# Start of a convolution and maxout kernel: wider weight transfers, one pass for the last 64 channels, and a new order of the opening work

## The chip, the cores and the metric

The kernel runs on one core of a Trainium2 chip. The metric is the device time of one execution in microseconds (us). Where a time stands with "at", it is counted from the start of the profiled span.

The engines are called as the profile calls them: PE (TensorE, matrix products; PEld is its loading of weights), ACT (ScalarE), DVE (VectorE), POOL (GpSimd) and SP (SyncE, which here issues almost all DMAs; its issues are listed as SPq).

## The reference

The input x holds 8 sequences of 4160 tokens with 192 channels. Each group of 24 channels (one head) is convolved along the sequence with its own 7 weights, the softmax of a row of `weight`, looking only backwards. Then every token goes through a feed-forward layer with three candidate products:

```python
w = softmax(weight)                                   # (8 heads, 7 taps)
x_pad = np.concatenate([zeros(B, 6, D), x], axis=1)
out = np.einsum('hk,bskhg->bshg', w, x_unf)           # causal convolution, x_unf: 7 shifted views
h = np.maximum(np.maximum(x @ w1, x @ w2), x @ w3)    # (33280, 768)
return h @ w_out                                      # (33280, 192)
```

All inputs and outputs are 4-byte floats. w1, w2 and w3 are 192 x 768 (590 KB each), w_out is 768 x 192.

## The kernel before

**The algebra.** With y the convolved tokens, max(y w1, y w2, y w3) is max(relu(y(w1-w3)), y(w2-w3)) + y w3. So two products per tile are needed instead of three: one with w1-w3 and one with w2-w3. The part y w3 goes through w_out together with the rest: a small matrix `m16` = w3 w_out is made once. The 192 channels are handled as three chunks of 64. The differences are kept in `wd` (line 305): `wd[:, 0]` and `wd[:, 1]` hold channels 0 to 127 of the two products, `wd[:, 2]` holds channels 128 to 191 of both (one in the lower 64 partitions, one in the upper), and a fourth part is made from the first two by `cross_wd` (L322), which moves 64 partitions to the other half. `make_wd` (L310) subtracts for two of the six 128-wide column groups j at a time.

**The blocks.** The tokens are cut into 65 blocks of 512. For the first four (the "dense" blocks) the convolution is done on PE by `conv_dense` (L376): 5 pieces of up to 103 tokens, each multiplied with a band matrix that holds the taps. From block 4 on, another form of the convolution is used, with transposing DMAs. This study is about the first 25 us; what follows is a steady loop over blocks 2 to 64 (L762).

**`conv_dense`.** The input of a dense block comes in as `xf` (one DMA for a block, two for block 0), is cast to 2-byte floats into `xz` by `cast_dense` (L207; two variants v, three casts each), and is multiplied by 32-channel slots: 4 slots are written beside each other into the 128 PSUM partitions. Pass n=0 does slots 0 to 3 (channels 0 to 127), pass n=1 does slots 4 and 5 (channels 128 to 191) twice, so that both halves of the partitions hold the result, and each pass is copied to `yd` in one copy. `cross` (L395) fills the rest of `yd` for blocks 2 and 3.

**The products of blocks 0 and 1.** `l1_dense` (L527) makes them in two parts. Part "F" multiplies channels 0 to 127 and needs `yd[:, 0]` and `wd[:, 0]`, `wd[:, 1]`. Part "H" multiplies channels 128 to 191 (the "third products") and needs `yd[:, 2]` and `wd[:, 2]`. A pair such as (0, 2), (0, 3) means block 0, column groups 2 and 3. `tops` (L545) then takes a relu on ACT (L500) and a maximum on DVE (L505), which together empty the PSUM tiles.

**The order.** The schedule is written by hand: each engine runs its own instructions in the order of the program text, and waits for the data that an instruction needs. PSUM tiles come from pools with a tag: `psp` ("p") and `psq` ("q") have two buffers each, `psw` ("w") four. A new tile in a pool waits until the tile two (or four) before it has been read.

**The transfers.** All of the opening loads stand in SP's queue (L241 to L250): block 0's x, then slices of the weights by `load_wa` (L227: channels 0 to 127 of w3, w1, w2, three DMAs) and `load_wb` (L231: channels 128 to 191, three DMAs with 64 rows each), block 1's x between them, then w_out and blocks 2 and 3. In order: x0, wa 0:256, wb 0:256, x1, wa 256:512, wb 256:768, wa 512:768, w_out, x2, x3.

**Where the weights are prepared.** `make_wd` of groups 0:2 on DVE (L692, L693, L700), of group 2:4 on DVE for n = 0, 1 (L710, L711) and on POOL for n = 2 (L705), of 4:6 on POOL (L707). `copy_w3` (L314) doubles the upper part of w3 into the other 64 partitions; `cast_w3` (L318) makes the 2-byte w3 that PE transposes in `transpose_w3` (L334). ACT copies the transposed result out (L341), then does one `cross_wd` (L729), its share of block 2's convolution (L393, L399), and the two copies of `make_m` (L349). `make_m` uses both "p" buffers, and the first product of block 2 (L517) takes the first of these two next.

**`zero_x`** (L131) clears rows of the input buffers that blocks 4 to 6 will use, on ACT unless another engine is named.

Of the kernel before, what the change touches and what calls it, by code (L numbers as in the profile page):

```python
# [19 lines left out]
GRP = 24  # L20
BAND_W = 128 + PAD
NBLK = 512
CHK = 103
HALF = P // 2
# [4 lines left out]
def kernel(  # L29
# [12 lines left out]
    nc = tc.nc  # L42
# [3 lines left out]
    H, KWs = weight.shape  # L46
# [193 lines left out]
    wos = const.tile([P, NJ, D], FP32)  # L240
    load_x(0)  # L241
    load_wa(slice(0, PW))
    load_wb(slice(0, PW))
    load_x(1)
    load_wa(slice(PW, 2 * PW))
    load_wb(slice(PW, DFF))
    load_wa(slice(2 * PW, DFF))
    nc.sync.dma_start(out=wos[:], in_=moe_w_out.rearrange("(j p) c -> p j c", p=P))
    load_x(2)
    load_x(3)  # L250
# [1 line left out]
    make_identity(nc, ident[:])  # L252
    ident16 = const.tile([P, P], FP16)
    nc.gpsimd.tensor_copy(out=ident16[:], in_=ident[:])
    idle = const.tile([P, NBLK], FP16)
    nc.vector.memset(idle[:], 0.0)
    def keep_warm(widths, pool, tag):
# [24 lines left out]
    nc.vector.reciprocal(out=wrec[:], in_=wrec[:])  # L282
    zero_x(4)
    nc.vector.tensor_scalar_mul(out=line[0:NHEAD, 31:31 + KW], in0=wexp[:, 0:KW], scalar1=wrec[:])
    for v in range(2):
        nc.vector.memset(xz[1][v][:], 0.0)
    cast_dense(0, (nc.vector.tensor_copy, nc.vector.tensor_copy))
    CUT = 28
    for lo, hi, copy in ((0, CUT, nc.scalar.copy), (CUT, WIN, nc.vector.tensor_copy)):
        bps = psq.tile([32, hi - lo + 3, NHEAD], FP32, tag="q", name=f"band_{lo}")  # L290
        for c in range(lo, hi):
# [4 lines left out]
        for a in range(4):  # L296
            copy(out=band[32 * a:32 * a + 32, :, 32 * a + lo:32 * a + hi],
                 in_=bps[:, 0:hi - lo, :].rearrange("p c h -> p h c"))
    zero_x(5)
    keep_warm((NBLK,) * 3, psp, "p")  # L300


# [70 lines left out]
            slots[t0] = ysp.tile([P, 2, nu, 2, D], FP16, tag="ys", name=f"ys_{t}")  # L373
        convs[t0] = G, heads[0]

    def conv_dense(t, copies, pools=((None, None),) * 2, order=(0, 1)):  # L376


        yd = dense[t] = ydp.tile([P, NC, NBLK], FP16, tag="yd", name=f"yd_{t}")
        for n in order:  # L380
            slots_ = ((0, 1, 2, 3), (4, 5, 4, 5))[n]
            pool, tag = pools[n]
            ps = (pool or psw).tile([P, NBLK], FP32, tag=tag or "w", name=f"D{n}_{t}")
            for (q, b, row_lo, rlen, lo, hi, cc) in chunks_of[t]:
                for v in range(2):
                    for g, s in enumerate(slots_):
                        h = (32 * s + 31 * v) // GRP
                        nc.tensor.matmul(  # L388
                            ps[32 * g:32 * g + 32, lo:hi],
                            lhsT=xz[t][v][0:rlen, q, 32 * s:32 * s + 32],  # L390
                            rhs=band[0:rlen, h, cc:cc + hi - lo],
                            start=(v == 0), stop=(v == 1), tile_position=(0, 32 * g))
            copies[n](out=yd[:, 2 * n, :], in_=ps[:])  # L393

    def cross(t, *copies):  # L395

# [294 lines left out]
    GP = nc.gpsimd.tensor_copy  # L691
    make_wd(0, 0, 2)  # L692
    make_wd(1, 0, 2)  # L693
    zero_x(6, 4, NR, nc.vector)
    conv_dense(0, (ACT, DVE))
    zero_x(6, 0, 4)
    for t in range(NDENSE, XBUF):
        load_x(t)
    copy_w3(DVE, 0, 2)
    make_wd(2, 0, 2)  # L700
    cast_dense(1, (GP, ACT), (1, 2, 0))
    l1_dense([(0, 0, PQ), (0, 1, PQ)], "F")
    cast_w3(0, 2)
    copy_w3(GP, 2, 6)
    make_wd(2, 2, 4, nc.gpsimd)  # L705
    for n in range(NC):
        make_wd(n, 4, 6, nc.gpsimd)  # L707
    cast_w3(2, 6)
    conv_dense(1, (DVE, ACT), order=(1, 0))
    make_wd(0, 2, 4)  # L710
    make_wd(1, 2, 4)  # L711
    cross_wd(0, GP)
    GP(out=wo[:], in_=wos[:])
    l1_dense([(0, 0, PQ), (0, 1, PQ)], "H")
    tops((0, 0), (0, 1))
    l1_dense([(1, 0, WW), (1, 1, WW)], "HF")
    tops((1, 0), (1, 1))
    l1_dense([(0, 2, PQ), (0, 3, PQ)], "FH")
    tops((0, 2), (0, 3))
    l1_dense([(1, 2, WW), (1, 3, WW)], "HF")  # L720
# [5 lines left out]
    tops((1, 4), (1, 5))  # L726
    transpose_w3((PQ[0], PQ[0], PQ[1]))
    cast_dense(3, (GP, GP))
    cross_wd(1, ACT)  # L729
    first_hidden(0)  # L730
    first_hidden(1)
    conv_dense(2, (ACT, DVE), (WW[0], PQ[1]))
    cast_x(4)
    cross(2, ACT, DVE)
    make_m(0)
# [26 lines left out]
    for t in range(2, NB):  # L762
        u = convs_at.get(t, NB)
        late = t > 2 and u < NB
        if t in (3, 4):
            double(t + 1)
        if t > 3:
            for v in range(casts.get(t - 1, 8) + 1, casts[t] + 1):
                cast_x(v)
        l1(t, 0)  # L770
        if t == 2:
            first_rest()
        elif t == 3:
            cast_x(8)
            nc.gpsimd.tensor_copy(out=m16[0:HALF, 2, :], in_=m16[HALF:P, 0, :])
            nc.gpsimd.tensor_copy(out=m16[HALF:P, 2, :], in_=m16[HALF:P, 1, :])
        if t > 3 and not late:
            op(lambda t=t: (store(t - 2, 0, 4, (nc.sync,)),
                            turn(t + 2, (2,)) if place(t + 2)[1:] in ((0, 4), (0, 5)) else None,
                            turn(t + 1, (4,)) if place(t + 1)[1:] == (0, 5) else None, load_on(t)))  # L780
        else:
            op(lambda t=t: store(t - 2, 0, 4, (nc.sync,)))
        cuts = ROOM if late else EVEN
        st2(t - 1, (cuts[0], cuts[0]))
        for j in range(1, NJ):
            l1(t, j)
            if late and j == 1:
                st2(t - 1, (cuts[0] + OWN + AHEAD, cuts[0] + OWN))
                meet()
                quad, second = u >= QUADS, u < QUADS or t == u - 3  # L790
                conv(u, WPWQ, range(4 * second, 4 * second + 4) if quad else range(NHEAD))
                for i in (0, 2):
                    evac(u, i)
                for i in (1, 3):
                    evac(u, i, nc.vector.tensor_copy)
                if second:
                    turn(u)
# [52 lines left out]
```

## Time and profile before

| | |
|---|---|
| median of 3 runs | 453.1 us (452.54, 453.10, 453.47) |
| the profiled execution | 452.5 us |
| its span | 450.7 us, so 1.8 us lie around the span |
| PE busy | 444.7 us (99%) |
| DVE, ACT, POOL busy | 356.5, 320.3, 204.0 us (79%, 71%, 45%) |
| granted clock of PE | 1.00 |
| DMA | 72.01 MB, mean 160 GB/s |

Three rows of the opening, as the timelines give them:

| engine | from | what |
|---|---|---|
| PE | 6.22 | block 0's convolution, 80 matmuls, 1.10 us |
| PE | 9.87 | block 1's convolution, after a wait of 0.61 us |
| PE | 11.10 | from here on PE is busy without a larger gap |

A line of a timeline has: start, time taken, engine, line of the kernel, operation, tile written <- tiles read, shape, count, and in brackets the idle time before it with what ended it. A busy PE is not a PE at its peak, since matmuls overlap and their ends are modelled. What matters for this study is which wait ends last in a given stretch.

### The profile page before, as it was taken

The numbers are of one execution on the slowest core, as the hardware profiler recorded it, in microseconds if no ns is written. First come the engines' busy times: TensorE is split into PE (matmuls) and PEld (weight loads), VectorE is DVE, ScalarE is ACT, GpSimd is POOL, SyncE is SP. The second block draws the span as 40 slices with busy tenths as digits, with TensorE's granted clock in tenths as the row PEclk, the third lists the DMA queues.
The fourth block names the chain that finished last, engine by engine and source line by source line (L and its number), as shares of the span: only waits on it lengthen the run. The fifth ranks groups of instructions, "written<-read, shape, count | busy, mean of one in ns | idle before, by whom it ended". The sixth has DMA issues, their size and how long they took to land.

```text
span 450.7 us, 18261 instructions
## 1 busy us (share of the span) xinstructions
PE 444.7 (99%) x7576; PEld 409.5 (91%) x7576; DVE 356.5 (79%) x610; ACT 320.3 (71%) x600; POOL 204.0 (45%) x234
## 2 busy tenths in 40 slices
PE   7999999999999999999999999999999999999997
PEld 4579999999999999999999999999999999999996
DVE  7778778878778787787887887887887887887775
ACT  7977677767677676776776777776776776776664
POOL 2874836556464524714724635526544545124000
PEclk9999999999999999999999999999999999999999
DMA  7978999495977759649559749769549566172123
GB/s 204 238 191 158 208 183 240 134 217 148 183 208 161 184 107 214 172 112 205 158 138 185 190 103 193 192 105 218 157 116 207 160 157 151 48 139 75 56 71 106
DMA packets 128242, 72.01 MB, mean 160 GB/s; under 512 B 52320, under 2 KB 127967, under 8 KB 128159
## 3 DMA queue, kind: packets, MB, share of 16 engines
q1 hardware_dynamic: 127999, 70.75, 68.8%
q8 instruction: 59, 0.97, 1.0%
q14 instruction: 24, 0.20, 0.2%
q10 hardware_dynamic: 160, 0.10, 0.1%
HBM read 33.28 MB, written 25.56 MB: 131 GB/s over the span
## 4 chain that ended last, share of the span: by engine, by line
PE 97%; DMA 1%; SPq 1%; issue 0%; DVE 0%; POOL 0%; POOLq 0%
PE po L582 36%; PE lq L517 32%; PE lp L517 22%; PE G L367 3%; PE lw L541 1%; DMA xf<-in_x_dram 1%; PE D L388 1%; PE lp L541 1%; PE po L613 0%; PE po L640 0%; SPq L233 0%; SPq L229 0%; PE pm L347 0%; PE lq L541 0%; SPq L167 0%; PE pt L338 0%
## 5 line engine op out<-in xcount | busy, mean ns | idle before, releaser
L582 PE MATMUL po<-wo,h 64*128 64x192 f16 x3024 | 331.7, 243 | 0.0
L505 DVE TENSOR_TENSOR h<-r,lq 128x512 f16<-128x512 f16 x384 | 263.0, 686 | 84.3 <-ACT r L500 74.3
L500 ACT ACTIVATE r<-lp 128x512 f16<-128x512 f32 x384 | 229.0, 597 | 113.4 <-PE lp L517 103.0
L517 PE MATMUL lp<-yp,wd 64*128 64x512 f16 x1098 | 295.6, 376 | 0.0
L517 PE MATMUL lq<-yp,wd 64*128 64x512 f16 x1098 | 295.5, 376 | 0.0
L582 PEld LDWEIGHTS <-h 64*128 64x128 f16 x3024 | 242.6, 94 | 5.5 <-issue 4.1
L517 PEld LDWEIGHTS <-wd 64*128 64x128 f16 x2268 | 181.6, 94 | 14.9 <-issue 0.2
L199 POOL CAST x<-xf 103x768 f16<-103x768 f32 x122 | 97.2, 825 | 112.4 <-DMA xf<-in_x_dram 108.9
L582 PE MATMUL po<-m,yp 64*128 64x192 f16 x720 | 140.3, 243 | 0.0
L430 POOL COPY yp<-yp 64x1536 f16<-64x1536 f16 (+1 forms) x70 | 90.9, 1298 | 87.3 <-DMA yp<-ys 62.3
L590 DVE TENSOR_TENSOR o<-a,po 128x384 f32<-128x384 f32 x126 | 69.0, 548 | 0.0
L582 PEld LDWEIGHTS <-yp 64*128 64x128 f16 x720 | 66.3, 94 | 0.1
L589 ACT COPY a<-po 128x384 f32<-128x384 f32 x126 | 59.5, 472 | 0.0
L407 ACT CAST ys<-G 128x480 f16<-128x480 f32 (+1 forms) x53 | 25.4, 530 | 9.5 <-PE G L367 9.5
L407 DVE CAST ys<-G 128x480 f16<-128x480 f32 (+1 forms) x53 | 30.2, 610 | 0.0
L367 PE MATMUL G<-x,band 39*32 39x240 f16 (+3 forms) x1024 | 16.5, 242 | 0.0
L367 PEld LDWEIGHTS <-band 39*32 39x32 f16 x1024 | 10.2, 91 | 4.6 <-issue 4.1
L517 PE MATMUL lq<-yd,wd 64*128 64x512 f16 x36 | 9.7, 376 | 0.0
L517 PE MATMUL lp<-yd,wd 64*128 64x512 f16 x36 | 9.7, 376 | 0.0
L541 PEld LDWEIGHTS <-wd 128*128 128x128 f16 (+1 forms) x48 | 3.1, 96 | 6.0 <-issue 2.8
L216 POOL CAST xz<-xf 112x160 f16<-112x160 f32 (+2 forms) x15 | 4.3, 330 | 7.9 <-DMA xf<-in_x_dram 7.8
L388 PEld LDWEIGHTS <-xz 112*32 112x32 f16 x320 | 3.9, 96 | 2.7 <-POOL xz L216 1.1
(79 smaller groups left out, 98.1 us busy)
## 6 DMA issues: line engine op xcount, KB each, us to landing
xf<-in_x_dram SPq DMA_DIRECT2D x113, 234.0 KB
out_dram<-o SPq DMA_DIRECT2D x62, 384.0 KB
wall<-in_moe_w_dram SPq DMA_DIRECT2D x12, 128.0 KB
xf<-in_x_dram SPq DMA_DIRECT2D x7, 204.8 KB
xf<-in_x_dram SPq DMA_DIRECT2D x3, 420.0 KB
yp<-ys SPq DMA_TRANSPOSE x70
out_dram<-o SPq DMA_DIRECT2D x5, 192.0 KB
wos<-in_moe_w_out_dram SPq DMA_DIRECT2D x1, 576.0 KB
```

The costliest lines, as they stand in the source:

```text
L199: nc.gpsimd.tensor_copy(out=x16s[t0][0:K, :, :, u, r, :].rearrange("p h j c -> p j h c"), in_=xf[0:K, 4 * r:4 * r + 4, :].rearrange("p j ( ...
L367: nc.tensor.matmul(G[2 * (k // per) + i][TOK * j:TOK * (j + 1), k % per, :], lhsT=band[row, h, HALF * i + LAP:HALF * i + KR], rhs=x16s[t0] ...
L388: nc.tensor.matmul(ps[32 * g:32 * g + 32, lo:hi], lhsT=xz[t][v][0:rlen, q, 32 * s:32 * s + 32], rhs=band[0:rlen, h, cc:cc + hi - lo], star ...
L407: copy(out=slots[t][:, i % 2, :, :, GRP * h0:GRP * (h0 + per)].rearrange("p u r (h c) -> p h (u r) c", c=GRP), in_=G[i][:].rearrange("p h ...
L430: nc.gpsimd.tensor_copy(out=yp[HALF * i:HALF * (i + 1), 1, :, :, :, :].rearrange("p i u k n -> p (i u k n)"), in_=yp[HALF * (1 - i):HALF * ...
L500: nc.scalar.activation(out=r[:], in_=ps[0][:], func=AF.Relu)
L505: nc.vector.tensor_max(out=hs[t][:, j, :], in0=r[:], in1=q[:])
L517: nc.tensor.matmul(ps[i][:], lhsT=w_of(i, c, j), rhs=y_all(t, i, c), start=(n == 0), stop=(n == NC - 1))
L541: nc.tensor.matmul(open_ps[t, j, i][:], lhsT=a, rhs=b, start=(t, j, i) not in begun, stop=(t, j, i) in begun)
L582: nc.tensor.matmul(ps[b0, i][:, s % 2, :], lhsT=a, rhs=b, start=first, stop=last)
L589: nc.scalar.copy(out=a[:], in_=ps[s - 1, 0][:])
L590: nc.vector.tensor_add(out=outs[t][:, s - 1:s + 1, :], in0=a[:], in1=ps[s - 1, 1][:])
```

## The change

1. **Transfers.** The order becomes x0, wa 0:256, x1, wb 0:768, wa 256:768, w_out, x2, x3. The same bytes come in 9 weight transfers instead of 12: wb in three DMAs of 197 KB (instead of 66 and 131 KB), the later wa in three of 262 KB (instead of six of 131 KB). x1 is ahead of all of wb.
2. **Third chunk once.** Pass n=1 of `conv_dense` multiplies slots 4 and 5 only once per piece; pieces 0 to 2 write the lower 64 partitions, pieces 3 and 4 the upper, in pairs. That makes 60 matmuls per block instead of 80. The two halves (309 and 203 columns) are then copied to `yd` in four copies of 64 partitions: each half once to its own partitions, once to the others (in block 1 the second is done by POOL from `yd`).
3. **Who does what.** `make_wd` of 2:4 and 4:6 is all on POOL; `cast_w3` is one cast of all columns, behind them; both `copy_w3` go to ACT; `cross_wd(0)` goes from POOL to ACT, next to `cross_wd(1)`. Block 1's casts go from POOL and ACT to DVE and POOL. `zero_x(5)` and `zero_x(6)` go from ACT (and DVE) to POOL, as do the memsets of `xz[1]` from DVE. The band's copies are cut at column 25 instead of 28 between ACT and DVE.
4. **Order.** Block 1's convolution stands directly behind block 0's F part in the text, its pass n=0 first; POOL's weight work stands behind it. Block 1's first pair is done "FH" instead of "HF". The loads of x4 to x6 stand later in the text.

```diff
@@ loads
     load_x(0)
     load_wa(slice(0, PW))
-    load_wb(slice(0, PW))
     load_x(1)
-    load_wa(slice(PW, 2 * PW))
-    load_wb(slice(PW, DFF))
-    load_wa(slice(2 * PW, DFF))
+    load_wb(slice(0, DFF))
+    load_wa(slice(PW, DFF))
@@ setup
+    for v in range(2):
+        nc.gpsimd.memset(xz[1][v][:], 0.0)
-    for v in range(2):
-        nc.vector.memset(xz[1][v][:], 0.0)
-    CUT = 28
+    CUT = 25
-    zero_x(5)
+    zero_x(5, eng=nc.gpsimd)
@@ conv_dense
-    def conv_dense(t, copies, pools=((None, None),) * 2, order=(0, 1)):
+    def conv_dense(t, copies, pools=((None, None),) * 2, order=(0, 1), dup=None):
+        ch = chunks_of[t]
+        FAR = (NQ + 1) // 2
         for n in order:
-            slots_ = ((0, 1, 2, 3), (4, 5, 4, 5))[n]
+            if n == 0:
+                units = [[(c, 0, (0, 1, 2, 3))] for c in ch]
+            else:
+                units = [[(c, 2 * (c[0] // FAR), (4, 5)) for c in ch[k::FAR]] for k in range(FAR)]
...
-            copies[n](out=yd[:, 2 * n, :], in_=ps[:])
+            if n == 0:
+                copies[0](out=yd[:, 0, :], in_=ps[:])
+            else:
+                far = ch[FAR][4]
+                for i, (lo, hi) in enumerate(((0, far), (far, NBLK))):
+                    own, other = (slice(HALF * k, HALF * (k + 1)) for k in (i, 1 - i))
+                    copies[1 + i](out=yd[own, 2, lo:hi], in_=ps[own, lo:hi])
+                    if dup is None:
+                        copies[1 + i](out=yd[other, 2, lo:hi], in_=ps[own, lo:hi])
+                    else:
+                        dup(out=yd[other, 2, lo:hi], in_=yd[own, 2, lo:hi])
@@ the hand-written order
     make_wd(1, 0, 2)
-    zero_x(6, 4, NR, nc.vector)
-    conv_dense(0, (ACT, DVE))
-    zero_x(6, 0, 4)
+    conv_dense(0, (ACT, ACT, DVE))
+    cast_dense(1, (DVE, GP), (1, 2, 0))
+    l1_dense([(0, 0, PQ), (0, 1, PQ)], "F")
+    copy_w3(ACT, 0, 2)
+    make_wd(2, 0, 2)
+    copy_w3(ACT, 2, 6)
+    zero_x(6, eng=nc.gpsimd)
+    conv_dense(1, (ACT, DVE, DVE), dup=GP)
+    for n in range(NC):
+        make_wd(n, 2, 4, nc.gpsimd)
+    l1_dense([(0, 0, PQ), (0, 1, PQ)], "H")
+    tops((0, 0), (0, 1))
+    l1_dense([(1, 0, WW), (1, 1, WW)], "FH")
+    tops((1, 0), (1, 1))
+    for n in range(NC):
+        make_wd(n, 4, 6, nc.gpsimd)
+    cast_w3(0, 6)
+    GP(out=wo[:], in_=wos[:])
     for t in range(NDENSE, XBUF):
         load_x(t)
-    copy_w3(DVE, 0, 2)
-    make_wd(2, 0, 2)
-    cast_dense(1, (GP, ACT), (1, 2, 0))
-    l1_dense([(0, 0, PQ), (0, 1, PQ)], "F")
-    cast_w3(0, 2)
-    copy_w3(GP, 2, 6)
-    make_wd(2, 2, 4, nc.gpsimd)
-    for n in range(NC):
-        make_wd(n, 4, 6, nc.gpsimd)
-    cast_w3(2, 6)
-    conv_dense(1, (DVE, ACT), order=(1, 0))
-    make_wd(0, 2, 4)
-    make_wd(1, 2, 4)
-    cross_wd(0, GP)
-    GP(out=wo[:], in_=wos[:])
-    l1_dense([(0, 0, PQ), (0, 1, PQ)], "H")
-    tops((0, 0), (0, 1))
-    l1_dense([(1, 0, WW), (1, 1, WW)], "HF")
-    tops((1, 0), (1, 1))
     l1_dense([(0, 2, PQ), (0, 3, PQ)], "FH")
...
     cast_dense(3, (GP, GP))
+    cross_wd(0, ACT)
     cross_wd(1, ACT)
     first_hidden(0)
     first_hidden(1)
-    conv_dense(2, (ACT, DVE), (WW[0], PQ[1]))
+    conv_dense(2, (ACT, DVE, ACT), (WW[0], PQ[1]))
@@ the loop, at t == 2
-                conv_dense(3, (ACT, DVE))
+                conv_dense(3, (ACT, DVE, ACT))
```

More of the change, by code (lines that the diff above doesn't have):

```diff
@@ L382, in conv_dense @@
             pool, tag = pools[n]
             ps = (pool or psw).tile([P, NBLK], FP32, tag=tag or "w", name=f"D{n}_{t}")
-            for (q, b, row_lo, rlen, lo, hi, cc) in chunks_of[t]:
+            for unit in units:
                 for v in range(2):
[L386 to L392, printed above, removed]
@@ L393, in conv_dense @@
-            copies[n](out=yd[:, 2 * n, :], in_=ps[:])
+                    for (q, b, row_lo, rlen, lo, hi, cc), g0, slots_ in unit:
+                        for g, s in enumerate(slots_, g0):
+                            h = (32 * s + 31 * v) // GRP
+                            nc.tensor.matmul(
+                                ps[32 * g:32 * g + 32, lo:hi],
+                                lhsT=xz[t][v][0:rlen, q, 32 * s:32 * s + 32],
+                                rhs=band[0:rlen, h, cc:cc + hi - lo],
+                                start=(v == 0), stop=(v == 1), tile_position=(0, 32 * g))
```

## The prediction

> **What bounds the kernel now.** I read the page's busy shares first: PE is busy 444.7 of 450.7 us. So nothing can be gained in the steady loop except by giving PE less to do; all else is in the opening. Then PE's timeline there:
>
> ```profile
> 6.22 1.10 PE L388 MATMUL D<-band,xz 112*32 112x103 f16 x80 [0.38 <-DVE band L297]
> 8.24 0.59 PE L541 MATMUL lp<-yd,wd 128*128 128x512 f16 x2 [0.91 <-ACT yd L393]
> 9.87 1.30 PE L388 MATMUL D<-band,xz 112*32 112x103 f16 x80 [0.61 <-POOL xz L216]
> 11.10 0.39 PE L541 MATMUL lp<-yd,wd 64*128 64x512 f16 x1
> ...
> 13.15 0.59 PE L541 MATMUL lp<-yd,wd 128*128 128x512 f16 x2
> ...
> 14.16 0.39 PE L541 MATMUL lp<-yd,wd 64*128 64x512 f16 x1
> ```
>
> PE waits three times and runs through from 11.10 (H of block 0) to the end. The chain of waits says why it is 11.10: x1 is issued at 5.05, lands at 9.36, is cast, and block 1's convolution follows.
>
> ```profile
> 5.05 4.31 DMA xf<-in_x_dram
> ```
>
> Why 4.31 us? The windows (last columns: granted clock, DMA share, GB/s):
>
> ```profile
> 3.50:5.50 2.00, 2.00 (x44) 1.32 (x41) 1.91 (x10) 1.82 (x4) 0.00 (x0) 1.00 0.80 226
> 5.50:7.25 1.75, 1.37 (x82) 0.95 (x80) 1.64 (x7) 1.71 (x3) 0.00 (x0) 1.00 0.72 103
> 7.25:9.25 2.00, 1.09 (x12) 0.38 (x4) 1.71 (x4) 1.75 (x3) 0.00 (x0) 1.00 1.07 343
> 9.25:12.50 3.25, 2.64 (x90) 1.52 (x90) 1.66 (x4) 2.34 (x6) 1.41 (x4) 1.00 0.92 252
> ```
>
> At 103 GB/s the engines are starved: SP needs 0.58 to 0.60 us for each of the three wb issues at 3.15 to 5.01, and each brings only 66 KB (some 110 GB/s).
>
> Two more views set what follows. POOL's timeline gives the price of a weight subtraction, 2.96 us for 4, the first 0.72 (DVE's row: 0.42):
>
> ```profile
> 13.38 2.96 POOL L312 TENSOR_TENSOR wd<-wall 128x256 f16<-128x256 f32 x4 [0.20 <-DMA wall<-in_moe_w_dram]
> 16.29 1.03 POOL L320 CAST w3h<-wall 128x1024 f16<-128x1024 f32 x1
> ```
>
> And ACT, from 17.38 to 25.49, has no idle time over 0.1 us:
>
> ```profile
> 17.38 1.08 ACT L500 ACTIVATE r<-lp 128x512 f16<-128x512 f32 x2 [0.26 <-PE lq L541]
> ...
> 19.80 1.60 ACT L341 CAST w3t<-pt 128x512 f16<-128x512 f32 x3
> 21.42 0.83 ACT L323 COPY wd<-wd 64x768 f16<-64x768 f16 x1
> 22.32 0.59 ACT L393 CAST yd<-D 128x512 f16<-128x512 f32 x1
> 22.93 0.62 ACT L399 COPY yd<-yd 64x512 f16<-64x512 f16 x1
> 23.46 0.71 ACT L349 CAST m<-pm 128x192 f16<-128x192 f32 x2
> ```
>
> The first of these last two copies ends at 23.76 and frees a "p" buffer; PE starts block 2's first product (L517) at 23.81. PE and ACT arrive together there: any ACT work added before it delays PE.
>
> **The change, part by part.**
>
> *x1 and the early order: 1.7 us early, but not on the path.* By the windows 448 KB are moved at 3.50, so x0 and the first wa (823 KB) are through at about 5.2; x1 (430 KB at 343 GB/s) at 6.4, and with the lag that x1 showed before (its last byte by volume at 8.3, landed 9.36) it lands near 7.4 instead of 9.36. Casts on DVE and POOL (before: 0.86 on POOL; DVE's six for block 0 took 0.92, so three 0.46) end by about 8.6 even one after the other. H also needs all of wb: 1843 KB, by volume at about 9, landed 9.4, plus 0.42 for `wd[:, 2]`. H can start at about 9.6 instead of 11.10. The cheaper setup (`zero_x(5)` 1.47 off ACT, memsets 0.92 off DVE, the band's cut) is under these waits: block 0's casts cannot start before x0 is there (before: 4.61, directly behind the memset), and nothing is charged or credited.
>
> *What is late next: wa 256:768, through POOL.* F of (0, 2) needs `wd[:, 0]` and `wd[:, 1]`, H `wd[:, 2]`, now all on POOL and none before the big wa has landed, w3, w1, w2 in that order. Behind x0 and the first wa 1806 KB must come. At 343 GB/s that takes 5.3 us, at 252 it takes 7.2; over 7.25 to 14.00 the windows (343, 252, then 205) average 268, 6.7 us. By volume the end is at 10.5 to 12.4; the lag before was 1.0 us for x1 and about as much for the weights. So w2 lands between 11.5 and 13.4; I take 12.4, nearer to the row in which wb was on its way too (252), and w1 0.9 earlier, 11.5. Then POOL does three subtractions: max(11.5 + 3 x 0.73, 12.4 + 2 x 0.73) + 0.1 = 14.0. H of (0, 2) starts at 14.0 instead of 14.16: **-0.2** (-1.1 to +0.7). Of the 1.5 us won at H of (0, 0) nearly all is waited away here. Queued behind the waiting subtraction on POOL are those of 4:6, the w3 cast, w_out's cast and the casts of blocks 2 and 3: 11.5 + 6 x 0.73 = 15.9, + 1.64 = 17.5, + 1.14 = 18.7, still ahead of PE's transposes (18.80 before) and `first_hidden` (19.55 before). SP waits for POOL's `zero_x` only behind x3, some microseconds later.
>
> *ACT ahead of block 2: +1.15.* The anchor is H of (0, 4) and the relu behind it at 17.38, which move with the -0.2. From there ACT gets `cross_wd(0)`: 0.83 + 0.02. Block 2's convolution adds two copies of 64 x 203. From PSUM copies of 512 and 192 columns (0.586, 0.313) a column costs 0.85 ns, so 0.32 each; neighbours overlap by 0.1 to 0.2 (the relus start every 0.49 and take 0.60), so 0.30 for both. The pair of copies of `make_m` ends its first at 23.76 + 1.15 - 0.2 = 24.7, and PE starts L517 then, +0.95 against 23.81.
>
> *PE's own share: -0.18.* 80 matmuls start within 0.90 us, four at a time every 45 ns. The new pass needs 6 groups of four (the last pair half empty) instead of 10: 0.18 less per block. For blocks 0 to 2 this lies under the waits above; for block 3 (at 26.34, PE without gaps) it counts. ACT's two extra copies there are covered by its idle 1.02 before 28.64; without that cover they would cost up to 0.3. If the pairs do not run beside each other the gain is 0.
>
> *The rest.* The four 64-partition copies of blocks 0 and 1 (ACT 0.41 each, DVE 0.36 each) and POOL's doubling are ahead of the 14.0 with over 1 us to spare. The later loads of x4 to x6 come no later, because the stream before them is not starved any more.
>
> Sum: -0.2 + 1.15 - 0.18 = **+0.75 us**. The profiled execution's 452.5 becomes 453.25; the median is 0.6 higher, so I forecast 453.8 against 453.1.
>
> **Where a rule and a row differ.** The forecast leaves PE idle from about 11.5 to 13. Before, gaps up to 0.91 left the granted clock at 1.00. The Trainium skill, "TensorE: Matmul & The Clock Gate", section "Why this matters for your kernels", wants no gaps over some 3 us, or the clock halves; by that rule a gap of 2 us is safe, and the trace shows no longer one than the first 1.23. The Trainium skill, "DMA: Bandwidth & Descriptors", section "Where 436 GB/s comes from", puts one core's limit from memory at 358 GB/s; at that the 1806 KB would take 5.0 us (an estimate), so the measured 343 is nearly all there is.
>
> **The rivals.**
>
> *Slower: the wide wa is the new wait (0.40).* Mechanism: one 786 KB delivery feeds three 0.73 us subtractions on one engine, where before the same weights came in two portions and DVE did two of the three at 0.42. If wb beside it holds the stream at 252 GB/s or less, w2 lands at 13.4, H starts at 14.96, and the sum is +0.8 + 1.15 - 0.18 = +1.8. It decides from a landing of w2 at about 12.6 on, where the sum passes +0.9. For it: 252 and 205 GB/s in the rows after 9.25. Against it: 343 where nothing starves, 320 at 14 to 16. Price 454.9.
>
> *Faster: the stream runs at its best (0.10).* w2 at 11.0: POOL is done at 12.55, ahead by 1.6, and the sum is -1.6 + 1.15 - 0.18 = -0.6; PE cannot be ready for that H before about 12.25 (11.10 - 9.6 = 1.5, and some 0.3 of own time), so -1.0 is the end. Price 452.3.
>
> *ACT is not the gate at 23.8 (0.15).* If L517's buffer does not wait for `make_m`'s copy, or ACT's copies overlap more, +1.15 falls away and conv 2's 0.18 counts too: -0.2 - 0.36 = -0.55, 452.5. Against it: 23.76 and 23.81.
>
> *Clock gate (0.03).* A gap twice as long as forecast could cost some 3 us at half clock (half of it lost): 455.3.
>
> *The third chunk is not made at half price* (pairs not side by side): +0.18 on the forecast, within it.
>
> **How the numbers follow.** Forecast and its neighbours within 0.9 us (0.32), slower rival 0.40, clock 0.03, faster 0.10, ACT not the gate 0.15. A measurement of this kernel can tell about 0.2%, 0.9 us, from no change. Of the third rival nearly all is within that, as of the forecast's; some of the faster rival is too, since it only touches -0.9. That makes faster 0.12, same 0.46, slower 0.42. The forecast alone reaches from -0.2 to +0.9; with the landing's ends and the rivals' prices the range is 452.3 to 455.1.
>
> **What would show it.** Right: x1's casts near 7.5; block 1's convolution before 9; PE idle before the products of (0, 2), released by POOL's `wd`; no starved window of 100 GB/s; ACT between w3t and the copies of `make_m` longer by 1.1, and PE's L517 released by ACT. Wrong: H of (0, 2) before 13 or after 15; L517 directly behind pm; a convolution of 60 matmuls that still takes 1.1 us; new idle time of PE beyond 30 us.

## The result, and the profile after

After takes 458.49 us (457.95 to 458.77, 4 runs), before 452.82 in the same call (452.47 to 453.47): ratio 1.0116, interval 1.0088 to 1.0143, **5.7 us slower**. The prediction said 453.8, at most 455.1. After's profiled execution took 458.42, span 456.6 against 450.7, of which PE is busy 445.6 (444.7 before): of the 5.9 us between the spans 5.0 are waits of PE and 0.9 more busy time, though it has 80 matmuls fewer.

All that is lost is lost ahead of 66 us. Taking the same relu in both traces and subtracting its start before from its start after gives the clock of the loss: +1.87 at the first (block 0's first products), +2.58 at those of slices 2 to 5, +4.20 at block 2's first, +4.96 behind block 3's convolution, +5.79 from 66 us to the end. So there are four pieces: 2.58 in the opening, 1.62 ahead of block 2, 0.76 at block 3, 0.83 at 65 us.

PE's timeline of after in the opening (start, us, engine, line, in the bracket the idle time before it and what ended it):

```profile
4.84 1.20 PE L291 MATMUL band<-ident,line 128*32 128x32 f16 x38 [1.04 <-DVE line L284]
5.97 1.46 PE L261 MATMUL idle<-idle 128*128 128x512 f16 x3
7.37 1.56 PE L392 MATMUL D<-band,xz 112*32 112x103 f16 x60
...
12.12 0.91 PE L392 MATMUL D<-band,xz 112*32 112x103 f16 x60 [1.85 <-DVE xz L216]
12.97 0.39 PE L555 MATMUL lp<-yd,wd 64*128 64x512 f16 x1
...
15.37 0.60 PE L555 MATMUL lp<-yd,wd 128*128 128x512 f16 x2 [0.21 <-POOL wd L310]
...
16.74 0.39 PE L555 MATMUL lp<-yd,wd 64*128 64x512 f16 x1
```

Block 1's convolution stands at 12.12 (9.87 before, "before 9" forecast), the products of (0, 2) at 16.74 (14.16, 14.0). There is a new wait of 1.04 ahead of the band's matmuls. Behind it the same three idle matmuls take 1.46 us instead of 0.97, and the first convolution of 60 takes 1.56, the second 0.91: PE is still slow. The clock's records grant full speed from 5.21 us on before, from 9.44 after.

What ended these waits stands on VectorE and POOL. First VectorE's line for the small operation ahead of the band in before:

```profile
3.46 0.22 DVE L284 TENSOR_SCALAR line<-wexp,wrec 8x7 f16<-8x7 f32 x1
```

then VectorE's timeline of after:

```profile
3.46 1.33 DVE L284 TENSOR_SCALAR line<-wexp,wrec 8x7 f16<-8x7 f32 x1
...
9.88 0.37 DVE L403 CAST yd<-D 64x203 f16<-64x203 f32 x1 [1.92 <-ACT yd L405]
...
10.56 1.42 DVE L216 CAST xz<-xf 112x160 f16<-112x160 f32 x3
```

and POOL's:

```profile
3.40 1.37 POOL L137 MEMSET xf<- 32x1536 f32 x1
...
10.21 1.37 POOL L137 MEMSET xf<- 32x1536 f32 x1
13.65 0.85 POOL L407 COPY yd<-yd 64x309 f16<-64x309 f16 x2 [2.08 <-DVE yd L403]
14.59 2.98 POOL L310 TENSOR_TENSOR wd<-wall 128x256 f16<-128x256 f32 x4
```

An operation on 8 x 7 numbers takes 1.33 us (0.22 before) and ends at 4.79, as POOL's memset ends at 4.77. The first cast of x1 does the same: it starts at 10.56 and ends at 11.68, 0.10 after POOL's second memset. The casts also start late: x1 has landed at 9.18, but VectorE first copies its half of the third chunk, which waits until ScalarE has copied the other (9.44 + 0.41 = 9.85, and VectorE starts at 9.88). On POOL the weights' subtractions start at 14.59, though w1 has landed at 12.91 and w2 at 13.56: the doubling for block 1 stands ahead and waits 2.08.

The windows of after (last columns: granted clock, DMA share, GB/s):

```profile
3.50:5.50 2.00, 0.96 (x27) 0.66 (x25) 2.00 (x7) 1.05 (x1) 1.26 (x1) 1.00 0.85 183
5.50:7.25 1.75, 1.75 (x24) 0.71 (x20) 1.20 (x6) 1.30 (x4) 0.00 (x0) 1.00 1.03 288
7.25:9.25 2.00, 1.82 (x62) 1.54 (x62) 0.71 (x2) 0.78 (x2) 0.00 (x0) 1.00 1.06 217
```

The starved stretch of 103 GB/s is gone, as forecast. (The clock column shows 1.00 where no record has come yet.) But with the wide wb in the stream the DMA engines are busy all the time (1.06) at 217 GB/s only, and x1 lands hardly earlier than before.

ScalarE ahead of block 2:

```profile
24.00 1.69 ACT L321 COPY wd<-wd 64x768 f16<-64x768 f16 x2
25.71 0.59 ACT L398 CAST yd<-D 128x512 f16<-128x512 f32 x1
26.32 0.32 ACT L403 CAST yd<-D 64x203 f16<-64x203 f32 x1
26.66 0.33 ACT L405 CAST yd<-D 64x203 f16<-64x203 f32 x1
27.01 0.62 ACT L413 COPY yd<-yd 64x512 f16<-64x512 f16 x1
27.65 0.54 ACT L347 CAST m<-pm 128x192 f16<-128x192 f32 x2
```

and PE's first product of block 2:

```profile
28.02 0.37 PE L531 MATMUL lp<-yd,wd 64*128 64x512 f16 x1 [1.88 <-ACT m L347]
```

From the start of the w3t copies to the end of the first m copy it is 3.96 us before and 5.59 here. PE's L531 waits 1.88 for that copy: ScalarE is the gate, as forecast, only longer.

### The profile page after: what moved, and what is told of

Same layout as the page of the kernel before. It is cut to its first block, busy times and chain, and to the rows that moved or that the text cites. A ratio compares the mean times of both kernels' runs of the same rounds, so it can differ in the third digit from the quotient of the medians.

```text
span 456.6 us, 18102 instructions
## 1 busy us (share of the span) xinstructions
PE 445.6 (98%) x7496; PEld 407.2 (89%) x7496; DVE 357.2 (78%) x611; ACT 320.9 (70%) x604; POOL 209.1 (46%) x239
## 4 chain that ended last, share of the span: by engine, by line
PE 94%; ACT 2%; DVE 1%; issue 1%; POOL 0%; ACTq 0%; POOLq 0%; DVEq 0%
PE po L596 36%; PE lq L531 31%; PE lp L531 22%; PE G L365 3%; ACT r L514 1%; PE po L654 0%; PE D L392 0%; ACT wd L321 0%; POOL wd L310 0%; ACT w3t L339 0%; PE lw L555 0%; PE idle L261 0%; DVE xz L216 0%; PE lp L555 0%; DVE line L284 0%
## 5 line engine op out<-in xcount | busy, mean ns | idle before, releaser
L531 PE MATMUL lp<-yp,wd 64*128 64x512 f16 x1098 | 295.8, 376 | 0.6 <-issue 0.6
L531 PE MATMUL lq<-yp,wd 64*128 64x512 f16 x1098 | 295.7, 376 | 0.0
L531 PEld LDWEIGHTS <-wd 64*128 64x128 f16 x2268 | 181.7, 94 | 17.9 <-issue 2.9
L531 PE MATMUL lp<-yd,wd 64*128 64x512 f16 x36 | 9.7, 376 | 1.9 <-ACT m L347 1.9
L531 PE MATMUL lq<-yd,wd 64*128 64x512 f16 x36 | 9.7, 376 | 0.0
L596 PE MATMUL po<-m,yd 64*128 64x192 f16 x36 | 5.9, 243 | 0.9 <-DVE o L604 0.6
```

The lines of the kernel that those rows point to most:

```text
L531: nc.tensor.matmul(ps[i][:], lhsT=w_of(i, c, j), rhs=y_all(t, i, c), start=(n == 0), stop=(n == NC - 1))
L596: nc.tensor.matmul(ps[b0, i][:, s % 2, :], lhsT=a, rhs=b, start=first, stop=last)
```

## The experiments

Medians against before in the same call (before: 453.05 to 453.23 there), with the ratio that is on record and its interval (it is not always the quotient of the medians: e4's is 1.0040, its medians give 1.0028); differences in the text are those of medians. There are two kinds, one thing undone in after and one part done alone in before; then comes a ladder between the two, in which each row adds something to the row above.

| Kernel | us | ratio to before |
|---|---|---|
| **Undone in after** (458.49) | | |
| zeros on ScalarE (e1) | 458.1 | 1.0103 [1.0078, 1.0128] |
| no doubling on POOL (e2) | 459.1 | 1.0126 [1.0104, 1.0147] |
| cross_wd(0) on POOL (e3) | 458.85 | 1.0123 [1.0101, 1.0145] |
| that, and one engine for the third chunk's copies (e6) | 457.43 | 1.0095 [1.0067, 1.0124] |
| idle matmuls in the gaps (e8) | 458.36 | 1.0110 [1.0095, 1.0125] |
| all of these but e8, and the old transfers (e11) | 456.43 | 1.0059 [1.0040, 1.0077] |
| **Done alone in before** | | |
| the nine transfers (e5) | 455.08 | 1.0039 [1.0024, 1.0055] |
| the third chunk (e4) | 454.48 | 1.0040 [1.0019, 1.0061] |
| the two groups of zeros on POOL (e10) | 453.39 | 1.0002 [0.9991, 1.0013] |
| **Ladder from before to after** | | |
| the order of work and who does what, without the rows below (e13) | 454.61 | 1.0035 [1.0017, 1.0053] |
| with w3's wide copy on ScalarE (e12) | 455.45 | 1.0042 [1.0029, 1.0056] |
| with the zeros on POOL, cross_wd(0) on ScalarE (e9) | 455.84 | 1.0044 [1.0025, 1.0063] |
| with the third chunk and its copies (e7) | 459.05 | 1.0120 [1.0089, 1.0151] |

The first theory was that the loss is the order of loads (the weights of (0, 2) late), ScalarE's chain, and copies that take turns. Its rival was POOL's memsets and the late clock. Neither alone held.

### Undoing one thing in after

**e1, the zeros on ScalarE.**

```
-    zero_x(5, eng=nc.gpsimd)
+    zero_x(5)
...
-    zero_x(6, eng=nc.gpsimd)
+    zero_x(6)          # behind conv_dense(0)
```

> The changed kernel with the two clearings zero_x(5) and zero_x(6) on ACT again, as in the kernel before, instead of POOL; nothing else. Theory 1 (POOL's memsets hold DVE up: the 8x7 TENSOR_SCALAR of L284 took 1.33 us beside one of 1.37, the first cast of x1 1.12 beside the other): L284 takes 0.22 again, the band matmuls start near 3.75 instead of 4.84, block 1's convolution starts near 10 instead of 12.12, POOL's doubling of yd ends before 13, its subtractions start when w1 has landed (12.9), H of (0, 2) at about 15.2 instead of 16.74, and the time falls by about 1.5 us to 457.0. Theory 2 (the wide transfers alone set the opening; the long DVE rows are waits for data): DVE's rows stay long and the time stays within 0.4 us of 458.5.

The 8x7 operation took 0.22 again, block 0's convolution stood at 6.02 with 0.91 us, block 1's at 10.25. Yet the time fell by 0.4 only: the products of (0, 0) now waited for the subtraction on VectorE, whose wb landed at 11.74, POOL's subtractions began at 13.95 behind the doubling, and the granted clock was halved from 12.33 to 15.74 (and once more from 29.40 to 32.81, in this profile). So the memset is the first gate of several that end close together.

**e2, block 1's four copies on VectorE, none doubled on POOL** (`conv_dense(1, (ACT, DVE, DVE))` without `dup=GP`).

> The changed kernel, block 1's four copies of the third chunk all on DVE, so that POOL has no doubling ahead of its weight subtractions. Theory 1 (POOL's subtractions stand behind the doubling, which waits for block 1's convolution): they start at the landing of w1, 12.9, instead of 14.59, H of (0, 2) starts at about 15.2 instead of 16.74, and the time falls by 1.0 to 1.5 us, less what the 0.8 us more on DVE cost. Theory 2 (the transfers are late and hold POOL): they still start at 14.5 or so and the time does not fall, or rises by up to 0.8 us.

No gain. POOL's timeline there says why: the first subtraction is 2.3 us earlier and now starts with the landing of w1 (12.16 there, 12.91 in after), and the next ones wait for w2, which landed at 14.55 (13.56 in after).

```profile
12.33 0.72 POOL L310 TENSOR_TENSOR wd<-wall 128x256 f16<-128x256 f32 x1 [1.33 <-DMA wall<-in_moe_w_dram]
14.62 3.64 POOL L310 TENSOR_TENSOR wd<-wall 128x256 f16<-128x256 f32 x5 [1.56 <-DMA wall<-in_moe_w_dram]
```

**e3, cross_wd(0) on POOL** behind the cast of w_out, and **e6**, that and `conv_dense(2, (ACT, DVE, DVE))`, `conv_dense(3, (ACT, DVE, DVE))`, so that VectorE makes all third-chunk copies there.

> The changed kernel with cross_wd(0) on POOL behind w_out's cast, as in the kernel before, instead of ACT. Theory (ACT's chain from the transposed w3 to make_m is the gate of block 2): PE's wait of 1.88 us at 28.02 shortens by 0.83 to 0.86 us and the time falls by 0.85 us to 457.6. Rival (another wait takes its place, because POOL's casts of block 2 come 0.9 us later and hold block 2's convolution): the wait moves ahead of the convolution at 24.13 and the time falls by less than 0.4 us.

> After, with cross_wd(0) on POOL and the two halves of the third chunk of blocks 2 and 3 copied by VectorE alone. Theory (ScalarE's chain ahead of block 2 is 1.63 us longer for cross_wd(0) and for copies that take turns with VectorE; both have to go at once): 1.0 to 1.6 us faster than after, 456.9 to 457.5; the wait ahead of block 2's maxout falls from 1.88 to 0.3 to 0.5 us, and the wait of 1.1 us of ScalarE in block 3's convolution goes. Rival (what ended that wait was not ScalarE's chain but something behind it): within 0.4 us of after.

Alone, taking 0.83 us off ScalarE does nothing: the wait ahead of block 2 fell from 1.88 to 1.71, and a wait of 0.71 ahead of ScalarE's halves of the third chunk took its place. They start 0.09 after VectorE's halves end, as in block 3 of after; the profile puts this wait down to PE's pm, which ended 0.03 before. With the turns gone too (e6) PE's wait is 0.21 (0.13 and 0.04 behind it), as the theory said, and the median is 1.1 us below after's. But the executions overlap (456.63 to 459.56, after 457.95 to 458.77), and in e6's trace blocks 2 and 3 lose 1.84 instead of 2.38 us, only 0.5 less: VectorE now makes all four copies of block 3, and PE waits 1.05 for it there (0.33 and 0.58 in after). The rest of that trace's lead is an opening 0.88 earlier, which this edit does not reach: x1 landed at 8.29 instead of 9.18, with the same transfers. So the theory holds for block 2's wait, and its figure of 1.0 to 1.6 us is not shown.

**e7, the old transfers in after.**

> After with the twelve transfers of before, in their order, everything else as changed. Theory 1 (the order of loads cost 2 us alone, and shares its gate, the weights of H(0,2), with block 1's convolution and POOL's order ahead of it): within 0.3 us of after, 458.2 to 458.8. Rival (the losses add up): 1.5 to 2.0 us faster than after, 456.5 to 457.0.

459.05 (457.19 to 459.73), a little above the range of theory 1, and in the trace no relu ahead of 66 us moves by more than 0.1 us. So after's order of loads costs nothing beside what else stands in after's opening, while alone in before (e5) it costs 2.0: the two hide each other.

**e8, idle matmuls** that leave no result in the kernel.

```
-    keep_warm((NBLK,) * 5 + (NBLK // 2, P // 2), psp, "p")
+    keep_warm((NBLK,) * 7 + (NBLK // 2, P // 2), psp, "p")
...
+    keep_warm((NBLK,) * 8, psw, "w")     # ahead of conv_dense(1)
...
+    keep_warm((NBLK,) * 8, psq, "q")     # behind make_m(1)
```

> After with idle matmuls that leave no result in the kernel: keep_warm two wider ahead of block 0's convolution, eight matmuls of 512 columns ahead of block 1's convolution and eight behind make_m, so that TensorE's gaps in the opening get short. Gate theory (after's clock is granted at 9.4 instead of 5.2 us and again taken away for 3.4 us in some executions, because of these gaps): full clock in the mean of every run, and 0.5 to 1.0 us faster than after, 457.5 to 458.0. Rival (the clock costs nothing, since weights and copies gate the opening): the same time as after, or up to 0.5 us longer for the matmuls added.

The clock did what the theory said: granted at 4.9 us, a mean of 1.00 in all four runs (after: 0.996 in two of four), and the opening 0.7 to 0.9 earlier in the profile. The time did not follow (458.36). In this profile PE stands still from 76.88 to 78.06 with nothing that releases it, and the loss against before grows from 4.1 to 5.5 us there. After has such a stop at 65.43:

```profile
65.99 0.37 PE L531 MATMUL lp<-yp,wd 64*128 64x512 f16 x1 [0.56 <-issue]
```

### One part alone in before

**e5, the nine transfers.**

> The kernel before with the new transfers alone: x0, wa 0:256, x1, wb 0:768, wa 256:768. Theory 1 (the order delivers wb and the big wa later than they are needed: in the changed kernel wb is complete at 11.9, w1 at 12.9, w2 at 13.6): H of (0, 0) starts near 12.5 instead of 11.10, F of (0, 2) near 14.1 instead of 13.15, and the time is 1.0 to 1.4 us over before. Theory 2 (the transfers are better or neutral, and only the new work on POOL, ACT and DVE costs): the time is within 0.4 us of before or up to 0.8 below.

x1 lands at 8.31 instead of 9.36, and nothing is won. PE's timeline of e5:

```profile
9.19 1.59 PE L386 MATMUL D<-band,xz 112*32 112x103 f16 x80
11.23 0.39 PE L539 MATMUL lp<-yd,wd 64*128 64x512 f16 x1 [0.45 <-DVE wd L310]
...
14.79 0.38 PE L539 MATMUL lq<-yd,wd 128*128 128x512 f16 x1 [0.84 <-DVE h L503]
```

The convolution is 0.7 earlier; the products of (0, 0) wait for the wide wb instead, and the wide wa holds VectorE's subtractions, behind which its h operations queue. It is a loss of some 2 us at the median, above the 1.0 to 1.4 expected.

**e4, the third chunk alone**, copied by one engine of each pair.

```
-    conv_dense(0, (ACT, DVE))
+    conv_dense(0, (ACT, DVE, DVE))
...
-    conv_dense(1, (DVE, ACT), order=(1, 0))
+    conv_dense(1, (DVE, ACT, ACT), order=(1, 0))
```

(and `(ACT, DVE, DVE)` for blocks 2 and 3).

> The kernel before with nothing but the dense convolutions' third chunk made once (ten groups of matmuls become six in each of the dense convolutions), its two halves copied by one engine of each pair, so that no two engines take turns at the third. Theory (the third chunk is worth its matmuls on TensorE and nothing else; what after loses, it loses by the order of loads and by copies that take turns): 0.2 us faster to 0.4 us slower than before, near 453. Rival (the third chunk itself, written once and copied in two 64-partition halves, is what after loses): 1.5 to 2.5 us slower than before, 454.5 to 455.5.

454.48, 1.25 slower: the theory missed, and the rival's lower end nearly holds. PE needs less for it (0.92 instead of 1.10), but four 64-partition copies take VectorE 1.69 us at block 2 where one of 128 x 512 took 0.69. In the profiled run (457.7, the slowest of the ten) one more thing came behind them, and a stretch of half clock from 27.12 to 30.54 behind that. VectorE's timeline, then POOL's:

```profile
24.77 0.37 DVE L407 CAST yd<-D 64x203 f16<-64x203 f32 x1
25.17 1.83 DVE L415 COPY yd<-yd 64x512 f16<-64x512 f16 x1
```

```profile
23.71 3.14 POOL L199 CAST x<-xf 103x768 f16<-103x768 f32 x4
```

The copy of `cross`, L415 here, takes 0.58 in before and 1.83 here; it ends at 27.00 and POOL's four casts, back to back, at 26.85. The other traces show that this is an extreme. The copy takes 0.29 where no cast of POOL runs beside it (e9, e11). In the 15 traces where it starts beside one it ends 0.14 or 0.15 after the end of a cast: in 13 of the first that ends behind its start (0.33 to 0.93 us in all, before's 0.58 among them), in e10 of the second (1.00), and only here of the third. Mostly POOL's next cast follows at once, and VectorE gets in all the same.

**e10, the zeros of xz[1] and zero_x(5) on POOL, in before.**

> The kernel before with the zeros of xz[1] and zero_x(5) on POOL, as after has them, and nothing else. Theory (a memset of POOL holds VectorE's next small instruction, and TensorE's gap ahead of the band matmuls then puts off its clock): L286's 8x7 operation takes over 1 us, the clock is granted near 9.4 instead of 5.2, block 0's convolution starts about 1 us later; 0.3 to 1.0 us slower than before, since loads gate the opening at 9.4 anyway. Rival (the hold came from something else in after): that operation takes 0.22 us, and the time is that of before within 0.3.

The hold is reproduced to a hundredth of a us:

```profile
3.46 1.34 DVE L286 TENSOR_SCALAR line<-wexp,wrec 8x7 f16<-8x7 f32 x1
```

and PE's band matmuls start at 4.85 again; block 0's convolution starts at 7.37 instead of 6.22 and takes 1.91 instead of 1.10. This trace has no record of the clock, so the grant near 9.4 that the theory names is not shown by it. The profiled execution lost 1.3 us in its span (452.0 against 450.7), but the median of ten is 453.39 against 453.19 and the interval holds 1: the hold is shown, its price alone is at most 0.6 us.

### Everything undone, and the ladder

**e11**, after with the changes of e1, e2, e6 and e7 together:

> After with every cost that the single experiments named undone together: the twelve transfers of before, the zeros on ScalarE, block 1's four copies on VectorE, cross_wd(0) on POOL, one engine for the copies of blocks 2 and 3. Left of the change: block 1's convolution ahead of block 0's third products, and the third chunk made once. Theory (these are all the costs, and they hide behind each other one by one): 453.5 to 455.0, since the third chunk's copies alone cost 1.2 in a kernel like before. Rival (a cost that nobody has named yet): over 456.

456.43: the rival, a cost not yet named. **e12** goes further and takes the old dense convolution too. What is left is the order, and with it who does what: all of `make_wd` 2:4 on POOL, both `copy_w3` on ScalarE, block 1's casts on VectorE and POOL, the memsets of `xz[1]` on POOL, the band's cut:

> As the repair of all named costs, and the dense convolution of before too (third chunk made twice, copied whole): left of the change is the order of work alone, with block 1's convolution ahead of block 0's third products. Theory (that order in itself costs nothing, its neighbours did): 452.6 to 453.8. Rival (the order itself costs, for the weights of the third products are then subtracted later): 454.5 to 456.

Still 2.3 slower, again in the rival's range. ScalarE's timeline of e12 names a cost:

```profile
9.60 0.40 ACT L316 COPY wall<-wall 64x256 f32<-64x256 f32 x1
12.33 0.62 ACT L316 COPY wall<-wall 64x512 f32<-64x512 f32 x1 [2.33 <-DMA wall<-in_moe_w_dram]
12.97 0.58 ACT L393 CAST yd<-D 128x512 f16<-128x512 f32 x1
13.45 1.09 ACT L500 ACTIVATE r<-lp 128x512 f16<-128x512 f32 x2
```

The 64x512 copy of w3 waits 2.33 us for its transfer, and block 1's copy out of PSUM, whose convolution PE has had done since 11.3, and block 0's relus queue behind it; PE idles 1.76. In before this copy stands on POOL. Behind that gap the clock was halved (windows of e12):

```profile
10.00:13.00 3.00, 1.64 (x84) 1.19 (x85) 1.15 (x3) 0.65 (x3) 1.57 (x3) 1.00 0.73 201
...
14.00:16.00 2.00, 2.00 (x8) 0.38 (x6) 1.28 (x2) 0.55 (x3) 1.06 (x2) 0.50 1.03 300
```

**e13** moves this one copy.

```
-    copy_w3(ACT, 2, 6)
...
-    for n in range(NC):
+    for n in range(2):
         make_wd(n, 2, 4, nc.gpsimd)
+    copy_w3(GP, 2, 6)
+    make_wd(2, 2, 4, nc.gpsimd)
```

> The order alone, with one thing moved: the 64x512 copy of w3 from ScalarE, where it stood ahead of block 1's first copy and block 0's relus and waited until 12.3 for the wide transfer's last part, to POOL behind the subtractions of the first two row blocks (where before has it, on POOL). Theory (that wait in ScalarE's queue is what the order alone cost): the wait of 1.76 ahead of the third products goes, H(0,2) starts near 14.5 instead of 17.7, and the time is 0.3 to 0.9 slower than before, 453.5 to 454.1, in place of 455.4. Rival (the order costs for the half-clock window or for the subtractions, which all stand on POOL): 454.8 to 455.6, no change.

```profile
9.60 0.40 ACT L316 COPY wall<-wall 64x256 f32<-64x256 f32 x1
10.79 0.58 ACT L393 CAST yd<-D 128x512 f16<-128x512 f32 x1 [0.80 <-PE D L388]
11.55 1.08 ACT L500 ACTIVATE r<-lp 128x512 f16<-128x512 f32 x2 [0.17 <-PE lq L541]
```

The wait is gone, the products of (0, 2) stand at 14.27, and the profiled execution is 0.5 behind before's to the end, as the theory said. The median, 454.61, lies above its range, and the granted clock says why: the six executions with a mean of 0.999 or 1.00 have a median of 453.85 (0.8 slower than before, in the range), the four with 0.992 to 0.996 took 455.3 to 456.7. So the two theories share it: 0.5 to 0.7 us for the copy (454.53 in e12 to 453.85, these executions alone, three against six; 0.5 when each is taken against before in its own call), and close to 2 us for a half-clock window where one falls. None of before's 29 executions in that call has a mean below 0.998, and one of its 44 in the other calls of the experiments has (0.996).

**e9** adds the zeros on POOL and ScalarE's cross_wd(0); the whole third chunk is then what is left to after.

> After with the twelve transfers of before and before's dense convolution, whose third chunk is made twice and copied whole (ScalarE the first, VectorE the second, no copies on POOL): what is left of the change is the new order of work, the zeros on POOL and cross_wd(0) on ScalarE. Theory (the new order with what it puts on POOL and ScalarE costs about 2.6 us in the opening less POOL's four copies, and 0.85 for cross_wd(0); the third chunk costs the rest by its copies): 455.5 to 457.0, which is 2.3 to 3.8 slower than before and 1.5 to 3 faster than after. Rival (the order of work is free, the third chunk costs it all): 453.0 to 454.0.

455.84, in the range, and 3.2 below e7. In after's order the third chunk costs 2.6 us in the profile (spans 454.0 and 456.6), of which 0.9 is e7's stop at 65 us. What is left, 1.7, is nearer to the 1.25 that it costs in before.

### The levers pulled the other way

Could x1 ahead make before faster? **e14** puts x1 ahead of the first third of wb and cuts the rest of wb in two; **e15** also moves ScalarE's zeros of 32x768 behind its casts of x1.

```
     load_x(0)
     load_wa(slice(0, PW))
-    load_wb(slice(0, PW))
     load_x(1)
+    load_wb(slice(0, PW))
     load_wa(slice(PW, 2 * PW))
-    load_wb(slice(PW, DFF))
+    load_wb(slice(PW, 2 * PW))
     load_wa(slice(2 * PW, DFF))
+    load_wb(slice(2 * PW, DFF))
```

> The kernel before with x1 ahead of the second weights' first third, those weights in three slices instead of two (fifteen transfers), and POOL's copy of w3 cut in two to match. Theory (TensorE idles 0.6 us ahead of block 1's convolution for x1, and works without a gap behind it; the wide second slice gates H(0,2)): x1 lands near 8.4 instead of 9.4, block 1's convolution starts near 9.3 instead of 9.9, H(0,2) near 13.6; 0.3 to 0.6 faster than before, 452.6 to 452.9. Rival (three more small transfers delay the weights by as much as x1 gains): within 0.3 of before, or up to 0.8 slower.

> As x1 first, and ScalarE's zeros of 32x768 (0.83 us), which stand ahead of its casts of x1, moved behind these casts. Theory: the casts start as x1 lands, block 1's convolution near 9.0; 0.5 to 0.9 faster than before, 452.3 to 452.7. Rival (its first copy of block 1 now stands behind these zeros, or the weights gate H(0,2) anyway): the same as x1 first alone.

Both lose: 455.39, ratio 1.0053 [1.0028, 1.0079], and 454.46, ratio 1.0022 [1.0007, 1.0037]. Block 1's convolution did start earlier (9.48 and 9.60 instead of 9.87), and by the relu of slice 4 of block 0 the lead had turned into +0.29 and +0.73. In e14's profile, 3.5 us longer than before's, one more stop without a releaser makes up 2.0: PE does 65 of the 80 matmuls of block 3's convolution, stands still for 1.79 until 30.26, and goes on with the other 15. No version here beats before.

## Why the prediction was wrong

**The step that failed: "H of (0, 2) starts at 14.0 instead of 14.16: -0.2".** It measured 16.74, +2.58. The step took one gate, the landing of wa. That landing came where the slower rival had it (w2 13.56, forecast 12.4, rival 13.4), and yet it set nothing: e7 takes the transfers back and no relu of the opening moves by 0.1. The subtractions started at 14.59 because three things that the prediction had waved through came first:

- "**nothing is charged or credited**" for the moved zeros. POOL's memsets held VectorE twice, for 1.1 us ahead of the band (gone in e1, made again in e10) and for 0.9 us in x1's casts (gone in e1).
- The four copies "**and POOL's doubling are ahead of the 14.0 with over 1 us to spare**". The spare was reckoned from a convolution before 9. The doubling stands ahead of the subtractions on POOL and waits for that convolution, at 12.12; and the copies of the two halves by ScalarE and VectorE do not run beside each other but in turn.
- **x1 near 7.4**: it landed at 9.18. By the windows some 1300 KB were moved at 7.25, enough for x0, the first wa and x1 (1253 KB), so the lag was 2 us and not 1.0. That wb was moved beside x1 and not behind it fits this; no run isolates it. With the same nine transfers x1 landed between 8.29 (e6) and 9.49 (e3, e8), and in the eight traces with the old twelve between 8.94 and 9.43: the lead of 2 us is in none. Nor was 343 GB/s "nearly all there is": after moved 365 from 12.50 to 14.00.

Without these three, w3's copy on ScalarE was next in e12: 1.76 us of PE's time that the prediction does not mention at all. The prediction asked what is late next on POOL, and not on ScalarE, whose queue had got a wait for a transfer ahead of the copy that PE needed.

**"ACT ahead of block 2: +1.15".** Right mechanism, released by ScalarE as said, but 1.63: cross_wd(0) 0.85 as charged, the two copies 0.70 where an overlap had made them 0.30, the rest smaller gaps. With both undone (e6) PE's wait there falls to 0.21; cross_wd(0) alone, half of it, was no gain (e3), since VectorE's turns were as late.

**"PE's own share: -0.18".** The 60 matmuls take 0.92 instead of 1.10: right. But block 3's turn, whose two copies on ScalarE the prediction has "covered by its idle 1.02", was +0.76: in conv 3 ScalarE's two copies start at 32.92, when VectorE's end (32.83), and PE waits 0.33 and 0.58 behind them. Where VectorE makes all four copies (e4, e6, e11) it waits 1.04 or 1.05 instead, so taking away the turns alone would not have brought it back.

**The clock**, given 0.03 and "a gap of 2 us is safe": the six traces with the wait of 1.04 ahead of the band grant full clock at 8.65 to 10.60, the ten without it at 4.81 to 6.86, and in e12 a gap of 1.76 was followed by a half-clock window. It is a part of the loss, 0.7 to 0.9 us in e8's profile; that it is not the bulk follows from e8's median, which stays.

**The last 0.83** at 65 us is a stop of PE that the profile gives no releaser for, and that the prediction has no term for. Five traces have one (after 0.56, e7 0.63, e2 0.43 at 80 us, e8 1.18 at 77, e14 1.79 at 28). What they share is the place: counted in the trace's records of PE's instructions, PE breaks off behind the 2241st in after and e7, the 2753rd in e2 and e8, the 961st in e14, and these numbers lie multiples of 256 apart. In each, PE goes on 1.43 to 1.62 us after the end of a 16 KB fetch of instructions (after: 64.50), which began 11 to 15 us after the one before it; a trace has 58 or 59 such fetches for some 15,100 of these instructions, about one for 256. So PE most likely waited for instructions. No run moves a fetch: that is read from the traces and not tested, and why a fetch comes late stays open.

Right were the reading that all turns on the opening, the end of the starved stretch, ScalarE as the gate of block 2, and that an earlier block 1 brings nothing by itself (e5, e14, e15). Two of the prediction's own signs of being wrong came: H of (0, 2) after 15, and new idle time of PE beyond 30 us. The forecast's sum lacked costs that stood in no row of before, since no queue there held such a wait.

## What to carry to other kernels

When work moves between engines, follow each receiving queue in order and ask of every instruction that waits for a transfer or for another engine what stands behind it; here four queues (VectorE, POOL, ScalarE, the copies in turn) each had one. Costs in an opening are parallel gates: undoing one showed nothing here (e2, e3, e7), so price a part by adding it to the clean kernel (e4, e5, e10) and close the sum with a ladder. And what was saved on TensorE by halves of 64 partitions was paid in copies: 0.18 us won, 1.0 us more on VectorE (e4, block 2).

## What the runs showed of the hardware

- **POOL holds some operations of VectorE.** A POOL memset of 1.37 us made an 8x7 operation of VectorE last 1.33 instead of 0.22 (after, e10) and a cast of x1 1.12 instead of 0.27 (after, e1), and beside POOL's casts a copy of 64x512 lasts 0.33 to 1.00, once 1.83 (e4), instead of 0.29 (e9). In each case VectorE ends 0.02 to 0.15 after an operation of POOL. Others are not held: beside POOL's two memsets of 0.90 from 1.61 to 3.34 in after, VectorE's memset of the band took 0.51 and its sum 0.15, as in before. The Trainium skill, "SBUF — State Buffer", section "SBUF: two separate sides", has a pair of ports that VectorE shares with GpSimd as an exclusive lock, the second comer blocked for the whole instruction; the trace agrees in that it is a full stop, for an instruction of POOL that only writes too.
- **Half-clock windows last 3.41 us.** Every one in the records of e1, e2, e3, e4, e11 and e12 that ends before the record does has this length, and the stretches of full clock ahead of and between them are whole multiples of it (3.41, 6.83, 13.65, 20.48). The Trainium skill, "TensorE: Matmul & The Clock Gate", section "Part 1: The HAM clock gate (the "warmup" mystery)", has a free-running window of about 3.4 us, which agrees. Its rule of no gaps over some 3 us (section "Why this matters for your kernels") was not enough here: in e12 PE was busy for 1.65 of the 3.41 us ahead of such a window and its longest gap was 1.76. The busy share does not settle it either: ahead of the seven windows PE was busy for 1.33 to 1.80 of 3.41 us, and in the first such stretch behind the grant in after (1.57) and e7 (1.66) as little without one.
- **Two engines that copy halves of one PSUM tile into one tile took turns**: the second started 0.03 to 0.09 us after the first had ended (after at 9.88 and 32.92). The profile names the other engine's copy as what ended the wait, so the program makes them wait for each other; whether the chip needs it no run shows.
